# A recurrence followed by two MLPs: a deeper first-MLP pipeline, recurrence operations bound to their tiles, and low weight halves formed in PSUM

## The chip, the cores and the metric

The kernel runs on one core of a Trainium2 chip. The metric is the device time of one execution in microseconds (us), here the median of several. A core has five engines that run their own instruction streams, each in its own order, and wait for each other by semaphores: PE (matrix products; its weight loads are shown apart as PEld), DVE (elementwise), ACT (activation functions, copies), POOL (elementwise, slower), and SP, which here only issues DMAs. PE's clock is granted at one of two levels, 1.2 or 2.4 GHz; the profile gives the mean granted share of a stretch (1.00 is 2.4 GHz throughout).

## What is computed

A complex diagonal recurrence over 768 positions (4 batches of 8 heads, width 48), then two MLPs over the 3072 tokens of width 384. The first has a rational function of its hidden layer (2048 wide), the second a SiLU gate (1536 wide).

```python
for t in range(S):                                   # S = 768, states D x D, D = 48
    new_re = ar * S_re - ai * S_im
    new_im = ar * S_im + ai * S_re
    S_re, S_im = new_re + k_t v_t^T, new_im
    y[t] = q_t S_re
x = y reshaped to (3072, 384)
h = x @ w_in                                         # 384 -> 2048
P = a0 + a1 h + a2 h^2 + a3 h^3
Q = 1 + |b0| |h| + |b1| h^2
x = (P / (Q + 1e-6)) @ w_out                         # 2048 -> 384
g, val = x @ w_gate, x @ w_val                       # 384 -> 1536
out = (silu(g) * val) @ w_out                        # 1536 -> 384
```

## The kernel before

The tokens are worked in six passes of 512. A pass `i` is one call of `moe`: **stage A** is the first MLP, a loop over 16 blocks `f` of 128 hidden rows (L202 to L237), **stage B** the second MLP, a loop over 12 blocks (L249 to L267). Every product is made of three fp32r products: each operand stands as a high half and a low half (`hi`, `lo`), and high by high, high by low and low by high are summed. So a block of A costs PE 9 matmuls of 512 columns to form `ph` (`up`, L175) and 9 to add to the three accumulators `acc` (`down`, L183: six with `hi`, then three with `lo`). A block of B costs 18 for `pg` and `pv` and 9 for `acc`.

Between `up` and `down` of a block of A stand, with `ph` in PSUM: ACT `w` = |b1 ph| (L211) and `u` = a3 ph + a2 (L212); DVE `w` (L218, called p below), `u` (L221), ACT |w| (L222), DVE `u` (L223); ACT `Ln` and `Exp` (L117) that make the reciprocal `r`; and then the division, `divide`: DVE `hi` (L228), `w` (L229), `u` (L230) and POOL `lo` (L231). `half` and `pend` are lists that hold a block back: with `HALF` = 1 a block's division is written in the next block's turn, ahead of that block's own L218, and its `down` one turn later; L220 orders p behind the division. A block of B has ACT Silu, DVE `z` (L261), ACT `hi` (L262), DVE `lo` (L265).

Beside this runs the work for the next passes. The recurrence of a pair of units (512 tokens) is `ew_seed`, `ew_scan`, `ew_q`, `ew_k`, 36 steps in all (`EW`), almost all of it on DVE; its results go to DRAM (`qs`) and come back as `st`. `at_pair` then makes the 512 tokens of the next pass out of them with small matmuls (`pk`, `pp`, `pgs`, `py`, `px`), which is called attention here. `tick` is called once a block and issues some of these steps. How many, is set by the tables `ENDS` (recurrence done by the end of A and of B, in units of 36 steps), `SPAN` (blocks of A over which A's share is spread), `AT` (blocks over which attention is spread) and `HOLD` (attention steps held for the end of A). A scheduler then orders each engine's instructions by written order, readiness and its own costs; an `order(later, earlier)` binds two instructions of one engine.

The weights come as float64 words. `narrow` (L134) makes high and low halves of a block of 768 columns: three DVE bit operations (`to_bits`), ACT `hi`, two ACT operations for a range test, DVE `lo` = x - hi (L141). The halves are used in pass 0 and stored (`w1s`, `w2s`); later passes load them (`stored`, L290) into buffers of one tag, six of them (`W_BUFS`). Nine of the 16 blocks of the first MLP are converted before pass 0 (`EARLY1`), between the steps of the first pair's recurrence and attention. Other buffers: `ps` has 5 PSUM banks for everything but `acc`; `u` and `w` have 3, `r`, `hi` and `lo` 2. Ln and Exp share one ACT table (`lnexp`), Silu has another (`silu`); the table is switched with ACT_TABLE_LOAD.

## Time and profile before

| | |
|---|---|
| device time, median of 3 runs | 1451.88 us (1448.75 to 1460.53) |
| the profiled execution | 1443.08 us, its span 1441.2 us |
| PE matmul busy | 1149.0 us, 80% of the span |
| DVE busy | 987.0 us, 68% |
| ACT busy | 699.1 us, 49% |
| POOL busy | 127.3 us, 9% |
| DMA, mean over the span | 181 GB/s |

The busy share is a mean over stages that differ, so the span is cut below into stages: the time before the first `ph` matmul, and then A and B of each pass, cut at the first `ph` and the first `pg` matmul of each pass, to whole us. Passes 0, 1, 2, 4 and 5 are cut in two, pass 3 is one stretch. A matmul's shown length is modelled and longer than the distance at which matmuls follow each other; where a rate is wanted, it is taken from start to start.

### The profile page before, as it was taken

Reading aid. Unit: us, or ns where it says so; the run is one execution under the profiler, and the core shown is the slowest. Engines: PE = TensorE matmul, PEld = TensorE weight load, DVE = VectorE, ACT = ScalarE, POOL = GpSimd, SP = SyncE. Lnnn points to the kernel's source line nnn. Section 1 sums busy time; section 2 is a strip of 40 time slices with the busy share of each in tenths; the row PEclk is TensorE's granted clock in tenths of the full one; section 3 lists DMA queues with packets and bytes.
Section 4 is the critical chain, followed back from the end, with each engine's and each line's share of the span. In section 5 each row is a group of like instructions: output and inputs, shape, how many; then the busy total and the mean of one; then the engine's idle time right before and its main releaser. Section 6 shows DMA issues by size and latency. Waiting matters only on the chain.

```text
span 1441.2 us, 15114 instructions
## 1 busy us (share of the span) xinstructions
PE 1149.0 (80%) x5314; PEld 916.1 (64%) x5314; DVE 987.0 (68%) x1601; ACT 699.1 (49%) x1081; POOL 127.3 (9%) x110
## 2 busy tenths in 40 slices
PE   0047268579996788997889997899988989977797
PEld 0047135358884576885677875777867778854486
DVE  5967997998877888438887358879266752266521
ACT  6263478665466643238443258443254542354412
POOL 0000011110001111001111001110001110021100
PEclk9996599669899999999888999899999999999899
DMA  5386477556677744777334975336864346533451
GB/s 227 110 232 206 175 252 246 191 187 224 204 248 245 250 138 130 231 239 227 115 112 136 282 225 161 115 100 201 274 195 146 116 151 195 180 109 131 132 175 47
DMA packets 128291, 261.51 MB, mean 181 GB/s; under 512 B 8016, under 2 KB 85072, under 8 KB 127440
## 3 DMA queue, kind: packets, MB, share of 16 engines
q1 hardware_dynamic: 128208, 260.47, 55.8%
q8 instruction: 44, 0.72, 0.2%
q14 instruction: 39, 0.32, 0.1%
HBM read 210.11 MB, written 50.33 MB: 181 GB/s over the span
## 4 chain that ended last, share of the span: by engine, by line
PE 50%; DVE 21%; ACT 17%; POOL 5%; DMA 4%; issue 3%; POOLq 0%; SPq 0%; ACTq 0%; DVEq 0%
ACT r L117 5%; POOL lo L231 5%; PE acc L190 5%; PE acc L186 5%; PE acc L187 4%; PE pg L179 4%; PE pg L180 4%; PE pg L181 4%; PE pv L179 3%; PE pv L180 3%; PE pv L181 3%; PE py L646 3%; DVE hi L228 3%; DVE u L230 3%; ACT u L212 3%
## 5 line engine op out<-in xcount | busy, mean ns | idle before, releaser
L186 PE MATMUL acc<-hi,wt 128*128 128x512 f32 x504 | 220.6, 438 | 69.0 <-DVE hi L228 68.8
L231 POOL TENSOR_TENSOR lo<-u,r 128x512 fp32r<-128x512 f32 x96 | 126.6, 1319 | 1229.8 <-DVE u L230 1088.1
L187 PE MATMUL acc<-hi,wt 128*128 128x512 f32 x504 | 212.3, 421 | 0.0
L190 PE MATMUL acc<-lo,wt 128*128 128x512 f32 x504 | 159.2, 425 | 59.4 <-POOL lo L231 58.9
L261 DVE TENSOR_TENSOR w<-pv,u 128x512 f32<-128x512 f32 x72 | 49.8, 691 | 190.8 <-PE pv L181 190.7
L186 PEld LDWEIGHTS acc<-hi,wt 128*128 128x128 f32 x504 | 102.5, 203 | 114.6 <-DVE hi L228 93.2
L179 PE MATMUL ph<-xh,wt 128*128 128x512 f32 x288 | 124.4, 432 | 49.0 <-ACT wt L138 35.7
L190 PEld LDWEIGHTS acc<-lo,wt 128*128 128x128 f32 x504 | 93.0, 198 | 105.6 <-POOL lo L231 90.8
L211 ACT ACTIVATE w<-ph,par 128x512 f32<-128x512 f32 x96 | 65.9, 686 | 157.5 <-DVE u L230 132.5
L228 DVE SCALAR_TENSOR_TENSOR hi<-u,par,r 128x512 fp32r<-128x512 f32 x96 | 71.9, 749 | 92.9 <-ACT r L117 92.4
L181 PE MATMUL ph<-xh,wt 128*128 128x512 f32 x288 | 119.0, 413 | 2.9 <-DVE wt L141 2.9
L180 PE MATMUL ph<-xl,wt 128*128 128x512 f32 x288 | 118.8, 412 | 0.0
L117 ACT ACTIVATE u<-pg 128x512 f32<-128x512 f32 x72 | 43.0, 598 | 154.9 <-PE pg L181 154.9
L187 PEld LDWEIGHTS acc<-hi,wt 128*128 128x128 f32 x504 | 103.1, 205 | 19.5
L262 ACT ACTIVATE hi<-w 128x512 fp32r<-128x512 f32 x72 | 45.4, 630 | 124.8 <-DVE w L261 124.5
L179 PEld LDWEIGHTS ph<-xh,wt 128*128 128x128 f32 x288 | 58.2, 202 | 72.6 <-ACT wt L138 38.9
L619 PE MATMUL pk<-ident,st 96*128 96x96 f32 x160 | 23.8, 275 | 92.5 <-DMA st<-qs 91.8
L212 ACT ACTIVATE u<-ph,par 128x512 f32<-128x512 f32 x96 | 74.7, 778 | 40.7 <-POOL lo L231 40.5
L179 PE MATMUL pg<-x1h,wt 128*128 128x512 f32 x216 | 89.0, 412 | 1.1 <-ACT x1h L122 1.1
L180 PE MATMUL pg<-x1l,wt 128*128 128x512 f32 x216 | 86.7, 401 | 0.0
L181 PE MATMUL pg<-x1h,wt 128*128 128x512 f32 x216 | 86.4, 400 | 0.0
L179 PE MATMUL pv<-x1h,wt 128*128 128x512 f32 x216 | 85.0, 393 | 0.0
(110 smaller groups left out, 2513.0 us busy)
## 6 DMA issues: line engine op xcount, KB each, us to landing
wt<-w1s SPq DMA_DIRECT2D x89, 768.0 KB, 4.4
wt<-w2s SPq DMA_DIRECT2D x60, 768.0 KB, 4.6
wt<-w2s SPq DMA_DIRECT2D x60, 384.0 KB, 4.1
raw<-in_w_p SPq DMA_DIRECT2D x28, 768.0 KB, 5.6
qs<-qp SPq DMA_DIRECT2D x24, 768.0 KB, 5.0
st<-qs SPq DMA_DIRECT2D x96, 192.0 KB, 5.1
w1s<-wt SPq DMA_DIRECT2D x16, 768.0 KB, 4.1
a<-in_a_p SPq DMA_DIRECT2D x6, 1536.0 KB, 8.9
```

Of the source, the lines that this page charges most:

```text
L117: i = act(*args, **kw)
L179: t_.matmul(ph, whi, xh[:, k, :], start=(k == 0), stop=False)
L180: t_.matmul(ph, whi, xl[:, k, :], start=False, stop=False)
L181: t_.matmul(ph, wlo, xh[:, k, :], start=False, stop=(k == KT - 1))
L186: t_.matmul(acc[m], wt[:, 0, c : c + 128], hi, start=st, stop=False)
L187: t_.matmul(acc[m], wt[:, 1, c : c + 128], hi, start=False, stop=False)
L190: t_.matmul(acc[m], wt[:, 0, c : c + 128], lo, start=False, stop=sp)
L211: act(w, ph, AF.Abs, scale=b1)
L212: act(u, ph, AF.Identity, scale=a3, bias=a2)
L228: stt(hi, u, a0, r, ADD, MUL)
L231: g_.tensor_tensor(lo, u, r, MUL)
L261: tt(z, pv, sg, MUL)
```

## The change

Three things are changed.

First, in A the division of a block is written behind the next block's own DVE work (`order(half.pop(0)(), formed)`), where it stood ahead of it, and `flush(gf)` leaves one block more between a division and its `down`. `hi` and `lo` are now taken from their buffers inside `divide`. p is ordered behind the last division (`divided[-1]`).

Second, `tt` and `stt` are wrapped (`held_back`, one line of the file, so all of DVE's tensor operations show as that line): while `tick` runs, each of them is ordered behind the DVE operation `formed` of the block in which it is issued. Before, the scheduler could run such an operation as soon as its inputs were there. `ENDS`, `SPAN` and `AT` are changed with it: in passes 1 to 3, B now ends with whole pairs done (3.0, 4.0, 5.0 where it was 2.8, 3.8, 4.8), and attention of passes 2 to 4 begins at block 1 of A.

Third, for the first MLP's weights the low half is formed by PE: in PSUM, x times the identity minus hi times the identity, 384 columns at a time, and ACT copies it to `lo`.

```diff
-ENDS = ((1.06, 1.5), (2.06, 2.8), (3.06, 3.8), (4.06, 4.8), (5.0, 5.0), (5.0, 5.0))
-SPAN = (16, 10, 5, 5, 5, 5)
-AT = ((16, 16, 0, 11), (10, 16, 0, 6), (4, 16, 0, 1), (4, 16, 0, 1), (4, 16, 0, 1), (4, 16, 0, 1))
+ENDS = ((1.06, 1.5), (2.06, 3.0), (3.06, 4.0), (4.06, 5.0), (5.0, 5.0), (5.0, 5.0))
+SPAN = (16, 11, 8, 8, 5, 5)
+AT = ((16, 16, 0, 11), (12, 16, 0, 6), (1, 16, 0, 1), (1, 16, 0, 1), (1, 16, 0, 1), (1, 16, 0, 1))
...
-    tt, stt, act = v_.tensor_tensor, v_.scalar_tensor_tensor, s_.activation
+    act = s_.activation
+    pin = {"on": False, "at": None}
+    def held_back(op):
+        def f(*args, **kw):
+            i = op(*args, **kw)
+            if pin["on"] and pin["at"] is not None:
+                order(i, pin["at"])
+            return i
+        return f
+    tt, stt = held_back(v_.tensor_tensor), held_back(v_.scalar_tensor_tensor)
...
+    minus = cpool.tile([128, 128], F32R, name="minus")
-    def narrow(raw, x, wt, low_sum):
+    def narrow(raw, x, wt, low_sum, ps=None):
...
-        tt(lo, xf, hi.bitcast(F32), SUB)
+        if ps is None:
+            tt(lo, xf, hi.bitcast(F32), SUB)
+            return
+        n = lo.shape[1]
+        for c in range(0, n, DM):
+            d = ps.tile([128, DM], F32, tag="ps", name="d")
+            t_.matmul(d, ident, xf[:, c : c + DM], start=True, stop=False)
+            t_.matmul(d, minus, hi[:, c : c + DM], start=False, stop=True)
+            act(lo[:, c : c + DM], d, AF.Copy)
...
-            hi, lo = mt("hi", F32R), mt("lo", F32R)
             act(w, ph, AF.Abs, scale=b1)
             act(u, ph, AF.Identity, scale=a3, bias=a2)
-            if len(half) > HALF - 1:
-                flush(0)
-                last = half.pop(0)()
-            else:
-                last = None
             p = stt(w, w, b0, ph, ADD, MUL)
-            if last is not None:
-                order(p, last)
+            if divided:
+                order(p, divided[-1])
             tt(u, u, ph, MUL)
             act(w, w, AF.Abs)
-            stt(u, u, a1, ph, ADD, MUL)
+            formed = stt(u, u, a1, ph, ADD, MUL)
...
-            def divide(f=f, wts=wts, u=u, w=w, r=r, hi=hi, lo=lo):
-                stt(hi, u, a0, r, ADD, MUL)
+            def divide(f=f, wts=wts, u=u, w=w, r=r):
+                hi, lo = mt("hi", F32R), mt("lo", F32R)
+                first = stt(hi, u, a0, r, ADD, MUL)
                 stt(w, w, 1.0 + EPS, hi.bitcast(F32), ADD, MUL)
-                last = stt(u, u, a0, w, ADD, SUB)
+                divided.append(stt(u, u, a0, w, ADD, SUB))
                 g_.tensor_tensor(lo, u, r, MUL)
...
-            tick(0)
+            tick(0, formed)
+            if len(half) > HALF:
+                flush(gf)
+                order(half.pop(0)(), formed)
         while half:
-            flush(0)
+            flush(gf)
             half.pop(0)()
...
-            tt(z, pv, sg, MUL)
+            formed = tt(z, pv, sg, MUL)
...
-            tick(1)
+            tick(1, formed)
...
-            narrow(raw, x, wt, bad_of)
+            narrow(raw, x, wt, bad_of, conv_ps[0] if src is w1_p else None)
...
+                pin["on"], pin["at"] = True, ins
                 cnt[ph] += 1
...
+                pin["on"] = False
```

How the instructions stand now is seen at three places. The first is DVE in A of pass 5, where no other work runs; numbers tell blocks apart. Before, the three operations of a division (`hi`, `w`, `u`) and the three of the next block (with `ph`) alternate, and a division uses the `u` of the block just formed:

```order
L218 SCALAR_TENSOR_TENSOR w_9035<-w_9035,par_90,ph_9022 128x512
L221 TENSOR_TENSOR u_9034<-u_9034,ph_9022 128x512
L223 SCALAR_TENSOR_TENSOR u_9034<-u_9034,par_90,ph_9022 128x512
L228 SCALAR_TENSOR_TENSOR hi_9037<-u_9034,par_90,r_9036 128x512
L229 SCALAR_TENSOR_TENSOR w_9035<-w_9035,hi_9037 128x512
L230 SCALAR_TENSOR_TENSOR u_9034<-u_9034,par_90,w_9035 128x512
```

In the changed kernel the division between the blocks 9131 and 9169 is that of the block before 9131 (`u_9105`); the one of `u_9143` comes after the next block:

```order
L87 SCALAR_TENSOR_TENSOR w_9144<-w_9144,par_90,ph_9131 128x512
L87 TENSOR_TENSOR u_9143<-u_9143,ph_9131 128x512
L87 SCALAR_TENSOR_TENSOR u_9143<-u_9143,par_90,ph_9131 128x512
L87 SCALAR_TENSOR_TENSOR hi_9163<-u_9105,par_90,r_9107 128x512
L87 SCALAR_TENSOR_TENSOR w_9106<-w_9106,hi_9163 128x512
L87 SCALAR_TENSOR_TENSOR u_9105<-u_9105,par_90,w_9106 128x512
L87 SCALAR_TENSOR_TENSOR w_9182<-w_9182,par_90,ph_9169 128x512
L87 TENSOR_TENSOR u_9181<-u_9181,ph_9169 128x512
L87 SCALAR_TENSOR_TENSOR u_9181<-u_9181,par_90,ph_9169 128x512
L87 SCALAR_TENSOR_TENSOR hi_9201<-u_9143,par_90,r_9145 128x512
```

The same six operations stand in the same proportion; what moved is which block a division belongs to.

The second is DVE in B of pass 2, at its third to sixth block: `w<-pv` is `z`, `lo` the low half, the rest is the recurrence. Before, this stretch held the last of it, and from the fifth block on B had none:

```order
L261 TENSOR_TENSOR w_5273<-pv_5249,u_5272 128x512
L531 TENSOR_TENSOR qp_5700<-q_5698,a_4421 128x8x6x16
L265 TENSOR_TENSOR lo_5275<-w_5273,hi_5274 128x512
L531 TENSOR_TENSOR qp_5700<-q_5698,a_4421 128x8x6x16
L531 TENSOR_TENSOR qp_5744<-q_5742,a_4421 128x8x6x16 x2
L567 TENSOR_TENSOR t6_5751<-t6_5751 128x8x96
L261 TENSOR_TENSOR w_5318<-pv_5294,u_5317 128x512
L567 TENSOR_TENSOR t6_5808<-t6_5808 128x8x96
L265 TENSOR_TENSOR lo_5320<-w_5318,hi_5319 128x512
L261 TENSOR_TENSOR w_5369<-pv_5345,u_5368 128x512
L265 TENSOR_TENSOR lo_5371<-w_5369,hi_5370 128x512
L261 TENSOR_TENSOR w_5416<-pv_5392,u_5415 128x512
```

In the changed kernel it is the beginning of the recurrence, and it goes on in this density to the last block:

```order
L87 TENSOR_TENSOR w_5391<-pv_5367,u_5390 128x512
L87 SCALAR_TENSOR_TENSOR t2_5358<-t1_4697,t2_5358 128x4x192
L87 TENSOR_TENSOR t3_5408<-a_4480 128x768
L87 TENSOR_TENSOR a_4480<-a_4480,t2_5358 128x1536
L87 TENSOR_TENSOR a_4480<-t3_5408 128x192 x2
L87 TENSOR_TENSOR lo_5393<-w_5391,hi_5392 128x512
L87 TENSOR_TENSOR t3_5408<-a_4480 128x768
L87 TENSOR_TENSOR w_5441<-pv_5417,u_5440 128x512
L87 TENSOR_TENSOR a_4480<-t3_5408 128x192 x2
L87 TENSOR_TENSOR t3_5408<-a_4480 128x768
L87 TENSOR_TENSOR lo_5443<-w_5441,hi_5442 128x512
L87 TENSOR_TENSOR a_4480<-t3_5408 128x192 x2
```

So nearly all of a pair's recurrence moved from A into B.

The third is ACT near the end of B of pass 2, where the recurrence needs Ln and Exp (`t6`) while B uses Silu (`u<-pg`). Before, they stood behind the last Silu of the pass, after the one table load that the next A needs anyway:

```order
L262 ACTIVATE hi_5682<-w_5681 128x512
L117 ACTIVATE u_5726<-pg_5706 128x512
L104 ACT_TABLE_LOAD
L117 ACTIVATE t6_5751<-t6_5751,cst_91 128x8x96
L117 ACTIVATE t6_5808<-t6_5808,cst_91 128x8x96
L262 ACTIVATE hi_5728<-w_5727 128x512
L117 ACTIVATE t6_5751<-t6_5751 128x8x96
L117 ACTIVATE t6_5808<-t6_5808 128x8x96
```

In the changed kernel they stand between the tenth and the eleventh Silu, with a table load ahead of them and one behind:

```order
L131 ACTIVATE u_5775<-pg_5751 128x512
L588 ACTIVATE t6_5793<-a_4480 128x1536
L588 ACTIVATE t6_5798<-a_4480 128x1536
L118 ACT_TABLE_LOAD
L284 ACTIVATE hi_5777<-w_5776 128x512
L131 ACTIVATE t6_5793<-t6_5793,cst_91 128x8x96
L131 ACTIVATE t6_5798<-t6_5798,cst_91 128x8x96
L131 ACTIVATE t6_5793<-t6_5793 128x8x96
L131 ACTIVATE t6_5798<-t6_5798 128x8x96
L118 ACT_TABLE_LOAD
L131 ACTIVATE u_5828<-pg_5808 128x512
```

Two loads are added by this in each of passes 1 to 3, six in all. On PE of pass 5 the `down` of a block stands about four blocks behind its `up`; in passes 2 to 4 three blocks.

## Rows read from the trace of the kernel before

**Rows 1.** Stretches: length; busy (count) of PE, PEld, DVE, ACT, POOL; clock; DMA share, GB/s.
```profile
0.00:163.00 163.00, 43.97 (x269) 43.15 (x270) 128.50 (x236) 75.10 (x106) 0.71 (x14) 0.87 0.57 191
163.00:309.00 146.00, 96.53 (x288) 63.41 (x288) 133.08 (x183) 101.13 (x153) 24.05 (x16) 0.76 0.66 220
309.00:422.00 113.00, 113.00 (x615) 97.77 (x615) 93.10 (x180) 63.64 (x118) 0.00 (x0) 0.90 0.60 202
422.00:558.00 136.00, 104.41 (x463) 78.89 (x461) 112.48 (x178) 81.28 (x120) 20.47 (x16) 0.91 0.64 211
558.00:640.00 82.00, 81.78 (x405) 68.95 (x405) 39.70 (x72) 23.69 (x37) 0.00 (x0) 1.00 0.70 214
640.00:778.00 138.00, 115.91 (x563) 92.69 (x561) 110.99 (x195) 78.49 (x125) 20.52 (x16) 0.90 0.47 150
778.00:850.00 72.00, 71.80 (x318) 59.47 (x319) 33.58 (x43) 21.57 (x33) 0.00 (x0) 1.00 0.77 237
850.00:1055.00 205.00, 186.22 (x912) 151.10 (x911) 147.05 (x246) 99.60 (x154) 20.50 (x16) 0.95 0.56 177
1055.00:1176.00 121.00, 106.14 (x549) 85.06 (x547) 83.68 (x120) 62.78 (x100) 20.53 (x16) 0.96 0.46 148
1176.00:1250.00 74.00, 73.78 (x328) 60.90 (x327) 18.96 (x28) 17.93 (x29) 0.00 (x0) 1.00 0.61 192
1250.00:1359.00 109.00, 81.57 (x291) 53.65 (x289) 67.26 (x96) 56.29 (x85) 20.52 (x16) 0.95 0.37 123
1359.00:1441.00 82.00, 73.87 (x326) 61.11 (x326) 18.65 (x28) 17.58 (x30) 0.00 (x0) 0.98 0.37 117
```
**Rows 2.** Timeline of pass 5, A, one block: start, length, instruction, [idle before <- releaser].
```profile
1330.84 0.75 DVE L228 SCALAR_TENSOR_TENSOR hi<-u,par,r 128x512 fp32r<-128x512 f32 x1 [2.20 <-ACT r L117]
...
1331.62 0.69 DVE L229 SCALAR_TENSOR_TENSOR w<-w,hi 128x512 f32<-128x512 f32 x1
...
1332.35 0.75 DVE L230 SCALAR_TENSOR_TENSOR u<-u,par,w 128x512 f32<-128x512 f32 x1
...
1333.02 0.74 DVE L218 SCALAR_TENSOR_TENSOR w<-w,par,ph 128x512 f32<-128x512 f32 x1
...
1333.27 1.27 POOL L231 TENSOR_TENSOR lo<-u,r 128x512 fp32r<-128x512 f32 x1 [5.22 <-DVE u L230]
1333.68 0.68 DVE L221 TENSOR_TENSOR u<-u,ph 128x512 f32<-128x512 f32 x1
1334.39 0.75 DVE L223 SCALAR_TENSOR_TENSOR u<-u,par,ph 128x512 f32<-128x512 f32 x1
...
1335.26 0.62 ACT L222 ACTIVATE w<-w 128x512 f32<-128x512 f32 x1
...
1336.66 0.63 ACT L117 ACTIVATE r<-r 128x512 f32<-128x512 f32 x1
1337.32 0.75 DVE L228 SCALAR_TENSOR_TENSOR hi<-u,par,r 128x512 fp32r<-128x512 f32 x1 [2.18 <-ACT r L117]
```

**Rows 3.** Timeline of PE in pass 3, A, a dense stretch; eight matmuls of 512 columns.
```profile
893.21 0.40 PE L180 MATMUL ph<-xl,wt 128*128 128x512 f32 x1
...
894.81 0.39 PE L181 MATMUL ph<-xh,wt 128*128 128x512 f32 x1
```

**Rows 4.** Waits in pass 5, A: who <- for whom: us in total, times, longest.
```profile
DVE hi L228 <- ACT r L117: 33.3, 16, 3.1
```

**Rows 5.** Waits in the first 163 us.
```profile
PE ph L179 <- ACT wt L138: 26.5, 1, 26.5
```

**Rows 6.** Weight loads of L290, all 209 of them, from issue to landing.
```profile
DMA to landing us min/median/max: 3.5/4.5/8.2
```

**Rows 7.** Groups by line and shape: count, busy us, mean ns, idle before.
```profile
L117 ACT ACTIVATE t<-t,cst 128x768 f32<-128x768 f32 x36 | 33.0, 930 | 1.7 <-DVE t L567 1.7
...
L141 DVE TENSOR_TENSOR wt<-raw,wt 128x768 fp32r<-128x768 f32 x28 | 26.7, 954 | 1.2 <-ACT wt L138 1.0
...
L104 ACT ACT_TABLE_LOAD x12 | 15.4, 1283 | 0.9 <-PEq L857 0.7
```

More of the change, by code (lines that the diff above doesn't have):

```diff
@@ L193, in mt @@
             return mp.tile([128, gf, T], dt, tag=tag, name=tag, bufs=M_BUFS.get(tag, 3))
-        pend, half = [], []
+        pend, half, divided = [], [], []
         def flush(n):
@@ L233, in divide @@
                     pend.append((acc, wts[j], DM, hi[:, j, :], lo[:, j, :], f + j == 0, f + j == F1 - 1))
-                return last
+                return first
             half.append(divide)
-            tick(0)
+            tick(0, formed)
+            if len(half) > HALF:
+                flush(gf)
+                order(half.pop(0)(), formed)
         while half:
-            flush(0)
+            flush(gf)
             half.pop(0)()
-        tick(2)
+        tick(2, None)
         flush(0)
@@ L309, in spans @@
         return [(c, min(2 * DM, src.shape[2] - c)) for c in range(0, src.shape[2], 2 * DM)]
-    ntiny = [0]
+    ntiny, conv_ps = [0], [None]
     def moe_pools(es):
@@ L417, in general @@
                     split(px, xh[:, :, cs], xl[:, :, cs])
-                moe(pools, 512, xh, xl, out[:, :, bass.ds(j * (UPB * 512) + k * 512, 512)], lambda ph: None, silu, feed(stored, pools[3]))
+                moe(pools, 512, xh, xl, out[:, :, bass.ds(j * (UPB * 512) + k * 512, 512)], lambda ph, ins: None, silu, feed(stored, pools[3]))
     with ExitStack() as es:
@@ L721, in tile_recurrence_moe @@
         lnexp()
+        conv_ps[0] = ps
         run(ew_seed(0))
+        nc.sync.dma_start(ident, ident_p)
+        act(minus, ident, AF.Copy, scale=-1.0)
         nc.sync.dma_start(mask, mask_p)
-        nc.sync.dma_start(ident, ident_p)
         nc.sync.dma_start(par[:, 0:4], ma.partition_broadcast(128))
@@ L749, in at_to, with tick @@
                     next(at, None)
-            def tick(ph, cnt=[0, 0], eb=eb, e0=e0, e1=e1, n=n, at=at, at_to=at_to, at_n=at_n, w=AT[i], i=i):
+            def tick(ph, ins, cnt=[0, 0], eb=eb, e0=e0, e1=e1, n=n, at=at, at_to=at_to, at_n=at_n, w=AT[i], i=i):
                 if ph == 2:
```

## Prediction

> **What bounds the kernel now.** I read the stretches first [rows 1], because the mean shares (PE 80%, DVE 68%) hide that the stages differ. B of pass 4 takes 74 us with PE busy 73.78 at clock 1.00 and DVE at 18.96: PE and nothing else. A of pass 5 has the same shape of work without company, and takes 109 us with PE 81.57 and DVE 67.26: neither engine is full. What a matmul of 512 columns costs at full clock comes from the dense stretch [rows 3]: seven distances in 1.60 us, 0.229 us each. So PE needs 324 x 0.229 = 74 us for a B, which it gets, and 288 x 0.229 = 66 us for an A, which takes 109 to 138.
>
> The timeline of A says why [rows 2]. From one `hi` to the next is 6.48 us, and it is one chain: `hi`, `w`, `u` of the division on DVE, then p (1333.02), then |w|, Ln and Exp on ACT (Exp ends 1337.29), then the next `hi` (1337.32). DVE stands 2.2 us before each `hi`; over the stage it waits 33.3 us for ACT's `r` in 16 waits [rows 4]. PE could do the block's 18 matmuls in 4.1 us. So A is bound by a latency loop between DVE and ACT, not by any engine. In passes 1 to 3 the recurrence sits on DVE in the same stage (111 to 112 us of 136 to 138 [rows 1]).
>
> **The deeper pipeline, bare (pass 5).** With the division one block behind, ACT's Abs, Ln and Exp run while DVE does the other block's division. The loop is then DVE's six operations at their distances [rows 2]: p 0.66, `u` 0.71, `u` to `hi` 0.67 (not shown in this order; taken as the distance from `u` to p, 0.67, and at most the dependent distance 0.78), `hi` 0.78, `w` 0.73, `u` 0.67: 4.22 us, against PE's 4.11. Sixteen blocks are 68 us, ahead of them about 3 (9 matmuls, 2.1, and a first ACT operation, 0.7), behind them about 5 (POOL `lo` 1.27 [rows 2], three matmuls 0.7, and the split of `acc`, two operations of some 0.7 twice over): 76 us where 109 stand. **Gain 33.** What is late next is the weights: the six buffers of the tag are now held for up to four or five blocks, so a load starts only when a `down` ends, and it has about one block of PE time to land. Landing takes 4.5 in the median and 8.2 at most [rows 6]. Two blocks cost at least a landing and a block of PE: (4.5 + 4.1)/2 = 4.3 us, nothing; with 8.2, 6.15 us a block and no more than 5 us gained in all. I take the median, since nothing else loads in pass 5 (0.37 of the DMA engines busy).
>
> **A of passes 2 to 4.** PE's attention work: pass 4's A has 258 matmuls more than pass 5's and 24.6 us more of PE [rows 1]. So PE needs 66 + 25 = 91 us. DVE's recurrence r and attention a: pass 2 has 36 steps and 144.6 us of DVE in A and B, pass 5 has neither and 85.9, pass 4 has a fifth of the steps and 102.6. So r + a = 58.7 and 0.2 r + a = 16.7; r = 52.5, a = 6.2. With two of 36 steps left in A, DVE needs 67.3 + 2.9 + 6.2 = 76 us. PE bounds, and with 2 us at the start and 7 for the tail and the waits of `pk` for `st` (the last products are now written at the end of B, shortly before they are read back), A takes 100. Below lies PE's 91, above 120, if attention's hand-overs between PE, ACT and DVE keep today's idle time. Gains: pass 2, 138 to 100, **38**; pass 3, whose A was 205 - 72 = 133, **33**; pass 4, 121 to 100, **21**.
>
> At this place the busy shares mislead. PE is shown busy 115.9 of 138 us in A of pass 2, which would leave 22 us to win; counted by starts 47 are left. By the busy time the idle of PE in the A stages of passes 1 to 5 is 32 + 22 + 19 + 15 + 27 = 115 us, less the 33 that B gives back below: 1361 us as profiled. The Trainium skill, "Perfetto Trace Analysis", section "Identifying the Most-Contended Engine", says that matmul busy share does not tell how near PE is to its limit and LDWEIGHTS share does. The trace agrees: PEld is busy 92.7 of 138 there, 45 us short [rows 1].
>
> **What B gives back.** B of passes 1 to 3 gets 34 of 36 steps, 49.6 us of DVE, on its own 18.7: 68 us against PE's 74. It fits, narrowly, but `z` and `lo` of a block now queue on DVE behind pieces of 4.1 us, and PE is only one block ahead. In addition Ln and Exp come between two Silus: two table loads of 1.28 and four operations of some 0.9 [rows 7], 6.2 us in which no `z` can start, against the 4.1 us of matmuls that PE has ready. I take 82 where 72 stand, **minus 10** each in passes 2 and 3. Bounds: 74, if all of it hides, and 123, if each piece is exposed (12 x (6.17 + 4.13)).
>
> **Pass 1.** A has 20 steps: DVE 67.3 + 29.2 + 3 = 99, and 11 for start and tail, 110 where 136 stand: gain 26. B has PE's 82 and some 6 more of attention, and DVE's 71: 95 where 82 stand. **Gain 13.**
>
> **The weights and pass 0.** DVE loses 16 operations of 0.954 [rows 7], 15.3 us. PE gains 32 pairs of 384 columns. A single pass is 0.17 us; if fp32 takes up to four passes at half clock, 1.4, and 0.2 to 0.3 for the other: 12 to 54 us in all, in stretches where PE is idle 119 and 50 us [rows 1]. ACT gains 32 copies of some 0.5 us (half the columns of the 0.93 operation), 16 us where it is busy 176 of 309. So these are hidden, unless PE's order puts them ahead of attention. For the gain: the stretch before the first `ph` ends with PE waiting 26.5 us for the first converted weights [rows 5], which queue on DVE behind the next pair's recurrence. Bound to its tiles, that recurrence no longer stands ahead of them. Against it: DVE has then less to fill its gaps before 163 us and more to do in A of pass 0, where it is busy 133 of 146. I set the two against each other: **0**, between 15 gained and 15 lost.
>
> **The sum** against the profiled 1443.1 us: 0 + 13 + (38 - 10) + (33 - 10) + 21 + 33 = 118, so 1325. The runs' median is 0.6% above that execution (1451.9), so I predict 1.006 x 1325 = **1333 us**.
>
> **The rivals.**
> *Loads or hand-overs take part of it* (chance 0.17). Six buffers are just enough, and landings near 8.2 would make pass 5's A 105 and cost pass 1 some 14: 1325 + 43 = 1368, 1376 on the runs' scale. The same result comes from A of passes 2 to 4 at 115. For it: the loads wait for `down` already today. Against: in passes 2 to 4 `down` is three blocks behind, which leaves a load two blocks and attention, some 11 us.
> *All of it hides* (0.15). B stays at PE's 74, that is 8 us better than taken in three passes, pass 0 gains 15, and A of 2 to 4 comes at 95: 1325 - 24 - 15 - 15 = 1271, 1279. For it: by DVE's sum there is room.
> *Slower* (0.04). The one mechanism is B of passes 1 to 3: if neither the pieces nor `z` and `lo` lie beside PE's matmuls, a block costs 6.17 + (49.6 + 18.7)/12 = 11.9 us and a B 142; three of them are 180 us over the forecast, 1513. It decides from about 124 us a B, where each recurrence piece is exposed whole. Against it: `ps` has five banks, and a block takes two, so PE works a block ahead.
> *The change does nothing* (0.02): the scheduler could have undone the order. The order of the built kernel shows the division a block later and the recurrence in B, so only a new wait of the same length in A could bring this.
>
> **How the numbers follow.** The forecast has 0.62, and its own bounds (95 to 108 for an A, 76 to 90 for a B, 15 either way in pass 0) reach from 1290 to 1370. To leave out no more than 2 in 10 the range goes to 1275 below, near the second rival, and to 1395 above, past the first. One per cent, about 15 us, is what a measurement of this kernel can tell from no change. Faster by more: 0.62 + 0.17 + 0.15 = 0.94; within 1%: 0.02; slower: 0.04.
>
> **What would show it.** In pass 5's A: `hi` waits for `r` no more, blocks follow at 4.2 to 4.4 us, clock near 1.00. In passes 2 to 4: PE waits for no `hi`, A near 100. In B of passes 1 to 3: DVE near 70 us of busy time, and waits of PE for `lo` and of ACT's Silu behind a table load; 82 us. The forecast is wrong if PE's first wait in A is for a weight load (above 5 us a block), if B exceeds 95, or if the first `ph` starts later than 163 us.

## The result, and the profile after

The changed kernel takes 1370.05 us (median of 4 runs, 1363.92 to 1378.43) where the kernel before took 1455.05 beside it: a ratio of 0.942, 95% interval 0.935 to 0.949. That is faster by 5.8%, inside the range of 1275 to 1395, 37 us above the number 1333 and 6 us from the first rival's 1376. The profiled execution took 1367.86 us, its span 1366.0.

The stretches of after, cut as [rows 1] at the first `ph` and the first `pg` of each pass. Columns: stretch, length; busy time and count of PE, PEld, DVE, ACT, POOL; granted clock; DMA share, GB/s.

```profile
0.00:167.80 167.80, 78.25 (x341) 56.74 (x342) 92.04 (x152) 77.71 (x120) 0.72 (x14) 0.75 0.60 202
167.80:345.20 177.40, 105.98 (x313) 71.59 (x311) 144.49 (x235) 104.84 (x160) 23.54 (x16) 0.73 0.47 151
345.20:453.20 108.00, 104.76 (x615) 89.89 (x616) 91.24 (x157) 72.18 (x130) 0.00 (x0) 1.00 0.73 252
453.20:575.50 122.30, 94.44 (x406) 74.61 (x405) 101.27 (x167) 77.52 (x117) 20.79 (x16) 0.87 0.65 211
575.50:662.30 86.80, 86.80 (x457) 74.20 (x458) 67.24 (x126) 29.50 (x42) 0.00 (x0) 1.00 0.60 192
662.30:769.80 107.50, 103.38 (x566) 88.39 (x565) 81.21 (x121) 74.15 (x122) 20.91 (x16) 0.94 0.63 207
769.80:841.40 71.60, 71.59 (x315) 58.81 (x316) 63.60 (x119) 27.07 (x37) 0.00 (x0) 1.00 0.69 219
841.40:956.30 114.90, 110.78 (x598) 95.98 (x596) 81.84 (x123) 74.41 (x120) 20.88 (x16) 0.90 0.57 179
956.30:1027.80 71.50, 71.48 (x315) 58.81 (x316) 64.48 (x125) 27.07 (x37) 0.00 (x0) 1.00 0.69 221
1027.80:1131.40 103.60, 100.84 (x550) 86.50 (x549) 79.43 (x117) 60.50 (x98) 20.84 (x16) 0.95 0.59 188
1131.40:1205.40 74.00, 73.97 (x328) 61.27 (x329) 18.96 (x28) 17.79 (x29) 0.00 (x0) 1.00 0.60 193
1205.40:1284.00 78.60, 69.73 (x290) 54.10 (x288) 65.75 (x97) 55.66 (x86) 20.94 (x16) 0.98 0.49 166
1284.00:1366.00 82.00, 73.81 (x326) 61.07 (x326) 18.60 (x28) 17.33 (x29) 0.00 (x0) 0.97 0.38 121
```

Read against [rows 1]: A of passes 1, 2, 4 and 5 lost 14, 31, 17 and 30 us (122.3 for 136, 107.5 for 138, 103.6 for 121, 78.6 for 109), pass 3 as a whole 19 (186.4 for 205). The recurrence has left A: DVE is busy 81 us there in pass 2 where it was 111, and 64 us in the B behind it where it was 34. B of pass 2 did not get longer (71.6 for 72), B of pass 1 did, by 5 (86.8 for 82). And one place lost: the first `pg` comes at 345 us where it came at 309. The change gained some 111 us behind that point and gave 36 back ahead of it.

The latency loop is gone exactly as worked out. A timeline of DVE in pass 5's A, one block (start, length, instruction), to be held against [rows 2]:

```profile
1240.16 0.75 DVE L87 SCALAR_TENSOR_TENSOR hi<-u,par,r 128x512 fp32r<-128x512 f32 x1
1240.94 0.69 DVE L87 SCALAR_TENSOR_TENSOR w<-w,hi 128x512 f32<-128x512 f32 x1
1241.67 0.75 DVE L87 SCALAR_TENSOR_TENSOR u<-u,par,w 128x512 f32<-128x512 f32 x1
1242.34 0.74 DVE L87 SCALAR_TENSOR_TENSOR w<-w,par,ph 128x512 f32<-128x512 f32 x1
1243.00 0.68 DVE L87 TENSOR_TENSOR u<-u,ph 128x512 f32<-128x512 f32 x1
1243.72 0.75 DVE L87 SCALAR_TENSOR_TENSOR u<-u,par,ph 128x512 f32<-128x512 f32 x1
1244.38 0.75 DVE L87 SCALAR_TENSOR_TENSOR hi<-u,par,r 128x512 fp32r<-128x512 f32 x1
```

From `hi` to `hi` are 4.22 us where 6.48 were, with no wait in any of the six rows. (All of DVE's two-input operations now have one line, L87, that of the helper that binds them; they are told apart by their tiles.)

What grew ahead of 345 us shows in the waits and groups. The waits of PE and of SP's queue in the first 168 us, PE's largest wait in A of pass 0, and the page's group of the first product for `d` (32 products; each of these shows as two instructions, so x64). Columns of a wait: us, times, longest; of a group: busy, mean ns | idle before:

```profile
PE d L163 <- DVE raw L87: 66.2, 9, 18.3
...
SPq L326 <- ACT wt L165: 85.8, 11, 13.8
...
PE acc L210 <- DVE hi L87: 40.9, 8, 8.9
...
L163 PE MATMUL d<-raw,ident 128*128 128x384 f32 x64 | 42.2, 774 | 71.2 <-DVE raw L87 69.4
```

PE works in order. While it stands before a `d` product, what is written behind it stands too; and SP's queue stands 86 us before the store of a converted block (L326), whose low half `d` must form first, with the next loads of raw words behind it. How much of the 66 us costs time is settled below: 53 of them lie ahead of the first attention product.

### The profile page after: what moved, and what is told of

It is laid out like the page before. It is cut to its first block, busy times and chain, and to the rows that moved or that the text cites. A ratio compares the mean times of both kernels' runs of the same rounds, so it can differ in the third digit from the quotient of the medians.

```text
span 1366.0 us, 15421 instructions
## 1 busy us (share of the span) xinstructions
PE 1145.8 (84%) x5410; PEld 932.0 (68%) x5410; DVE 970.2 (71%) x1585; ACT 715.7 (52%) x1120; POOL 128.6 (9%) x110
## 4 chain that ended last, share of the span: by engine, by line
PE 66%; DVE 16%; DMA 7%; ACT 7%; issue 3%; POOL 1%; SPq 0%; POOLq 0%; ACTq 0%; DVEq 0%
PE acc L214 7%; PE acc L210 7%; PE acc L211 7%; PE pg L203 4%; PE pg L205 4%; DMA wt<-w1s 4%; PE pg L204 4%; PE pv L203 4%; PE pv L204 4%; PE pv L205 3%; DVE t L87 3%; PE py L668 3%; PE ph L203 3%; PE pp L645 3%; PE ph L204 3%
## 5 line engine op out<-in xcount | busy, mean ns | idle before, releaser
L210 PE MATMUL acc<-hi,wt 128*128 128x512 f32 x504 | 217.1, 431 | 53.4 <-DVE hi L87 53.4
L211 PE MATMUL acc<-hi,wt 128*128 128x512 f32 x504 | 210.8, 418 | 0.0
L214 PE MATMUL acc<-lo,wt 128*128 128x512 f32 x504 | 155.1, 416 | 23.3 <-POOL lo L250 23.3
L203 PE MATMUL ph<-xh,wt 128*128 128x512 f32 x288 | 119.1, 414 | 32.2 <-DMA wt<-w1s 26.8
L87 DVE TENSOR_TENSOR w<-pv,u 128x512 f32<-128x512 f32 x72 | 49.6, 689 | 126.9 <-PE pv L205 112.7
L214 PEld LDWEIGHTS acc<-lo,wt 128*128 128x128 f32 x504 | 97.6, 199 | 52.3 <-POOL lo L250 31.6
L87 DVE SCALAR_TENSOR_TENSOR w<-w,par,ph 128x512 f32<-128x512 f32 x96 | 71.5, 744 | 63.6 <-ACT u L235 63.5
L205 PE MATMUL ph<-xh,wt 128*128 128x512 f32 x288 | 115.9, 402 | 0.0
L163 PE MATMUL d<-raw,ident 128*128 128x384 f32 x64 | 42.2, 774 | 71.2 <-DVE raw L87 69.4
L203 PE MATMUL pg<-x1h,wt 128*128 128x512 f32 x216 | 85.9, 398 | 3.5 <-ACT wt L154 2.0
L235 ACT ACTIVATE u<-ph,par 128x512 f32<-128x512 f32 x96 | 74.3, 774 | 20.2 <-POOL lo L250 20.1
L205 PE MATMUL pg<-x1h,wt 128*128 128x512 f32 x216 | 84.3, 390 | 0.3 <-DVE wt L87 0.3
```

Source lines behind the costliest of these rows:

```text
L87: i = op(*args, **kw)
L203: t_.matmul(ph, whi, xh[:, k, :], start=(k == 0), stop=False)
L205: t_.matmul(ph, wlo, xh[:, k, :], start=False, stop=(k == KT - 1))
L210: t_.matmul(acc[m], wt[:, 0, c : c + 128], hi, start=st, stop=False)
L211: t_.matmul(acc[m], wt[:, 1, c : c + 128], hi, start=False, stop=False)
L214: t_.matmul(acc[m], wt[:, 0, c : c + 128], lo, start=False, stop=sp)
```

## The experiments

All stages below are cut like the ones above, in us, each from one profiled execution; "to `pg` 0" is the time up to the first `pg` of pass 0. The first two rows are the two kernels, the others the experiments that change the parts. In the expectations and below, TensorE is PE, VectorE is DVE and ScalarE is ACT.

| kernel | to `pg` 0 | B0 | A1 | B1 | A2 | B2 | A3 | B3 | pass 4 | pass 5 |
|---|---|---|---|---|---|---|---|---|---|---|
| before | 309.0 | 113.4 | 135.9 | 81.7 | 138.2 | 71.9 | 133.5 | 71.9 | 194.9 | 190.8 |
| after | 345.2 | 108.0 | 122.2 | 86.9 | 107.5 | 71.6 | 114.9 | 71.5 | 177.5 | 160.6 |
| depth alone | 300.7 | 109.5 | 122.3 | 81.7 | 116.3 | 71.9 | 118.3 | 71.9 | 180.4 | 161.2 |
| depth, tables | 299.4 | 106.4 | 124.8 | 89.2 | 112.4 | 71.9 | 123.1 | 74.3 | 176.5 | 160.2 |
| depth, tables, bound in 2, 3 | 300.2 | 106.3 | 118.7 | 87.6 | 98.9 | 71.6 | 117.9 | 71.5 | 174.6 | 161.4 |
| after, lows on DVE | 319.9 | 109.6 | 122.4 | 86.9 | 107.5 | 71.6 | 114.9 | 71.5 | 174.4 | 161.4 |
| after, not bound | 328.7 | 106.6 | 106.2 | 87.9 | 112.2 | 71.9 | 121.0 | 74.5 | 171.3 | 160.6 |
| after, bound from pass 1 | 333.8 | 110.0 | 121.0 | 86.9 | 107.5 | 71.6 | 117.9 | 71.5 | 177.6 | 162.0 |
| after, old division | 338.6 | 114.1 | 125.6 | 86.9 | 115.9 | 71.6 | 120.9 | 72.2 | 190.5 | 190.5 |
| before, lows on PE | 325.9 | 112.1 | 124.9 | 83.3 | 134.0 | 71.9 | 138.7 | 71.9 | 193.5 | 192.3 |

**The first part undone.**

```diff
+            if half:
+                flush(0)
+                half.pop(0)()
             p = stt(w, w, b0, ph, ADD, MUL)
...
-            if len(half) > HALF:
-                flush(gf)
-                order(half.pop(0)(), formed)
```

> The changed kernel with its first part undone: in A the division of the block before stands again ahead of p, `down` follows it at once, and `hi` waits for `r` one block earlier; binding, tables and TensorE's low halves stay. My theory (the latency loop between VectorE and ScalarE bounded A, 6.48 us a block): A of pass 5 goes from 79 back to 105 to 110, A of passes 2 to 4 from 104 to 115 back to 112 to 125 (16 blocks at 6.5 to 7), pass 1 some 10 us longer: total 1410 to 1450. Rival (the recurrence's move out of A is what brought passes 2 to 4, and TensorE's attention work there fills the loop's gaps): only pass 5 loses 30 us, passes 1 to 4 stay within 5 us each, total 1390 to 1405.

Measured: 1433.63 us, ratio to before 0.990 (0.987 to 0.994). So without the deeper division binding, tables and TensorE's low halves together bring 1% (13 us), and the division is worth 64 us on top. The waits of DVE in A of pass 5 and of pass 2 show the old loop back:

```profile
DVE hi L87 <- ACT r L131: 33.3, 16, 3.3
...
DVE hi L87 <- ACT r L131: 24.0, 15, 4.4
```

The first line is [rows 4] again, the sum to the tenth, and A of pass 5 is 108.6 us. My theory holds in passes 2 to 4 (A of 116 to 121) and in pass 5. It missed pass 1, whose A is 3 us longer where some 10 were expected. The rival (attention fills the loop's gaps) does not hold: A of passes 2 to 4 is 6 to 13 us longer, not within 5.

**The first part alone.** The kernel of the separate losses (below) with the three old tables.

```diff
-ENDS = ((1.06, 1.5), (2.06, 3.0), (3.06, 4.0), (4.06, 5.0), (5.0, 5.0), (5.0, 5.0))
-SPAN = (16, 11, 8, 8, 5, 5)
+ENDS = ((1.06, 1.5), (2.06, 2.8), (3.06, 3.8), (4.06, 4.8), (5.0, 5.0), (5.0, 5.0))
+SPAN = (16, 10, 5, 5, 5, 5)
(AT likewise)
```

> The kernel before with the deeper division alone: old tables, no recurrence bound, low halves on VectorE. Question: what does the first part bring by itself, and what the new tables bring on top (that kernel, with the new tables, took 1339 us). Theory (the recurrence in A is VectorE's load there and must leave before the deeper division pays): pass 5 gains its 30 us, passes 2 and 3 gain 10 to 20 each (VectorE's 111 us in A are then the bound), pass 1 10, total 1355 to 1385. Rival (depth alone brings it, the tables nothing): 1332 to 1348.

Measured: 1331.10 us, 0.916 (0.912 to 0.920), 1 us below the rival's range. On the total the rival was right and my theory wrong: the deeper division alone does it, and the rest of the change takes some 39 us of that away again (1370.05 less 1331.10, each beside its own runs of before). By stages the theory was nearer than by its total: A of passes 2 and 3 gained 22 and 15 us, where it said 10 to 20; it had left out A of pass 4 (15) and the stretches up to A of pass 1 (12). What the new tables alone bring on top is unclear: with them the kernel took 1338.86 us, and the intervals overlap. A of pass 2 of this kernel:

```profile
614.20:730.50 116.30, 103.69 (x564) 85.22 (x562) 101.93 (x146) 77.39 (x126) 21.77 (x16) 0.94 0.57 181
```

DVE still carries 102 us there. That is more than after's 81, but it is under PE's 104, so it mostly hides, and the recurrence need not leave A for the division to pay. The two parts overlap, though: with the old division, binding and tables took A of pass 2 from 138 to 116 us as well. That is why the division is worth 118 us alone and only 64 on top of the rest.

**The third part undone.**

```diff
-            narrow(raw, x, wt, bad_of, conv_ps[0] if src is w1_p else None)
+            narrow(raw, x, wt, bad_of, None)
```

> The changed kernel with its third part undone: the 32 low halves of the first MLP's weights are formed by one subtraction each on VectorE again, and TensorE has no `d`. Question: where do the 31 us come from that pass 0 lost (first `ph` at 168 instead of 163, A 177 instead of 146). Theory P (the `d` matmuls stand in TensorE's order behind `down` and ahead of the next `ph`, so that conversion and VectorE go in lock-step): pass 0 comes back by 15 to 30 us, first `ph` at 160 to 165, total 1337 to 1352. Rival R (the recurrence that is bound to its tiles leaves VectorE idle before the first `ph` and loads it in A): VectorE only gets 15 us more to do, pass 0 is 5 to 20 us longer, total 1371 to 1386. Passes 1 to 5 the same to 2 us by both.

**The second part undone.** (The binding holds whatever VectorE does within a `tick`, attention's operations too; these runs do not part the two. Up to B of pass 0 only recurrence is issued there.)

```diff
-                pin["on"], pin["at"] = True, ins
+                pin["on"], pin["at"] = False, ins
```

> The changed kernel without the binding of the recurrence to its tiles (the order that each `tick` puts on VectorE's recurrence operations is never set); order of the division, tables and TensorE's low halves as changed. Theory R (the bound recurrence is pass 0's loss): first `ph` near 163, A of pass 0 near 150, 25 us gained there; and in passes 1 to 3 the recurrence slides out of B back into A, where VectorE's gaps are, and A of passes 2 and 3 becomes 10 to 20 us longer each: total 1350 to 1385. Rival P (TensorE's `d`): pass 0 stays at about 345 us to the first `pg`, total 1375 to 1410. Third view (the tables alone place the recurrence, the binding does little): passes 1 to 5 the same to 3 us each.

**The second part from pass 1 on**, with `i > 0` in that place.

> The changed kernel with the recurrence bound to its tiles only from pass 1 on, so that VectorE may fill the stretch before the first `ph` and pass 0 with recurrence as before. Theory R: A of pass 0 comes from 177 to about 150 and the first `ph` to 163 or less, total 1336 to 1350. Rival P (TensorE's `d` in the conversion): pass 0 stays within 8 us of the changed kernel's, total 1358 to 1370. If both bear a part, between them, 1350 to 1358.

**The second and third part undone together.**

> The changed kernel without its second and third part together: VectorE forms the low halves, no recurrence is bound, the deeper division and the new tables stay. Theory S (the two losses are separate and add up: TensorE's low halves cost 26 us and the binding 22, as each alone showed): first `ph` and A of pass 0 together 300 to 312 (before 309, changed 345), A of pass 1 near 106, total 1315 to 1330. Rival O (both cost the same thing, the lock-step of conversion and attention before the first `ph`, and one undone has undone it): 1338 to 1348.

Measured: lows on DVE 1343.76 us, 0.929 (0.923 to 0.934); not bound 1348.35, 0.932 (0.928 to 0.936); bound from pass 1 1354.16, 0.934 (0.929 to 0.939); both undone 1338.86, 0.923 (0.917 to 0.928). Each of the four is faster than the change by its median; for the second and third the interval touches that of the change (0.935 to 0.949). Of three of them, the stretches before the first `ph` and A of pass 0, in the order lows on DVE, not bound, both undone:

```profile
0.00:149.00 149.00, 37.81 (x268) 37.15 (x268) 94.55 (x155) 61.67 (x89) 0.71 (x14) 0.92 0.61 207
149.00:320.00 171.00, 101.65 (x289) 67.13 (x289) 156.01 (x248) 106.03 (x160) 24.67 (x16) 0.72 0.52 173
```
```profile
0.00:186.40 186.40, 81.84 (x340) 58.95 (x341) 140.24 (x249) 96.83 (x144) 0.71 (x14) 0.71 0.58 195
186.40:328.70 142.30, 94.81 (x313) 67.64 (x312) 119.07 (x183) 92.30 (x144) 27.25 (x16) 0.80 0.56 184
```
```profile
0.00:162.60 162.60, 43.79 (x269) 42.96 (x269) 128.15 (x236) 75.30 (x107) 0.71 (x14) 0.87 0.56 191
162.60:299.40 136.80, 94.65 (x288) 65.16 (x288) 130.04 (x175) 97.99 (x150) 25.71 (x16) 0.76 0.70 229
```

These, with after's two rows, make a square, read at the first `pg`. With TensorE's low halves: 345.2 bound, 328.7 unbound. With VectorE's: 319.9 and 299.4. So the low halves on PE cost 25 us (bound) or 29 (unbound), the binding 16 or 20, and the two add up to within 4 us. The binding's part is DVE's: it keeps some 34 us of recurrence out of the stretch before the first `ph` (94.6 us of DVE instead of 128.2). The first `ph` comes 13 us earlier for it, as I had argued, and A of pass 0 then holds 156 us of DVE in 171 and is 34 us longer. TensorE's part shifts the first `ph`, from 149 to 168 or from 163 to 186. Two waits of the first of the three kernels, in its first 149 us, show what PE's idle time there is made of:

```profile
PE pk L641 <- DMA st<-qs: 91.6, 1, 91.6
...
SPq L326 <- DVE wt L87: 62.5, 8, 12.5
```

With the low halves on DVE, PE's idle time ahead of attention is one wait, for the first `st`; behind it attention runs in one piece, and then PE waits 18.8 us for the first `ph`. With `d`, five of PE's nine waits for DVE (53 of the 66 us) lie in the place of that first wait and cost nothing: the first `pk` starts at 88.5 us, where it starts at 91.6 without `d`. The loss comes behind it, where the last of the early blocks are converted between the pieces of attention (`CV`). From the first `pk` to the end of the last `px`, with `d` (the changed kernel) and without (its low halves on DVE):

```profile
88.49:146.28 57.79, 47.47 (x287) 42.59 (x288) 17.86 (x25) 21.55 (x39) 0.00 (x0) 0.71 0.63 198
91.62:130.57 38.95, 37.80 (x268) 37.12 (x268) 14.64 (x21) 13.03 (x25) 0.00 (x0) 0.93 0.66 203
```

PE is busy 9.7 us longer, which is the products of `d` (9.6 us there; attention's own take 38 in both), and idle 9.2 us longer. These 19 us are the whole delay of the first `ph` (18.4 us); A of pass 0, which has `d` of its own, is another 7 longer. The clock of the second row, 0.93, can't be right and is no other cause: eight `pp` take 1.97 us up to 107 us in that kernel and 1.08 behind, the same two lengths as in the changed one. The stores that SP's queue puts ahead of the next loads wait 86 us instead of 70 (the 62.5 shown and one of 7.0 put down to another DVE operation).

Of the expectations, theory P was right for the low halves on DVE (25 us, total 1344), though the first `ph` came at 149 us, earlier than the 160 to 165 that it gave. For the binding the total fell just below the lower end given, and I was wrong about the place: the first `ph` went to 186, not to 163, since the lock-step with `d` stays; A of passes 2 and 3 grew by 5 and 6 us, not 10 to 20, and A of pass 1 shrank by 16, which no theory had. Bound from pass 1 on, the kernel lies where both bear a part, 1354, and its stretches say the same: the first `ph` at 193.9, late by `d`, and A of pass 0 139.8, as without binding. For "both undone" theory S holds up to the first `pg` (299.4 us for 300 to 312), but the total came as rival O said, because A of pass 1 went the other way: 124.8 instead of the 106.2 of the unbound kernel.

**The third part alone, on the kernel before** (old division, old tables, nothing bound).

> The kernel before with the third part alone: TensorE forms the low halves of the first MLP's weights and ScalarE copies them; old division, old tables, nothing bound. The step of my prediction that is tested: the 64 `d` pairs are hidden in TensorE's idle time of the first 309 us (119 and 50 us), so nothing. Theory P (TensorE works in order; its `d` wait for the converted bits, and attention stands behind them): first `ph` 15 to 25 us later, first `ph` and A of pass 0 together 325 to 340 instead of 309, total 1465 to 1480. Rival H (hidden, as forecast; the loss came only with the rest of the change): within 6 us of 1450.

Measured: 1450.91 us, 1.003 (0.999 to 1.007): no difference. Each theory was right about half of it. The first `ph` is 27 us late, at 189.5, and the first `pg` 17 us late, as P said; the end is not late, as H said. The first two stretches, and A of pass 1:

```profile
0.00:189.50 189.50, 85.11 (x340) 62.28 (x341) 142.48 (x251) 96.72 (x144) 0.72 (x14) 0.62 0.58 192
189.50:326.00 136.50, 93.59 (x314) 62.63 (x313) 121.05 (x209) 94.89 (x148) 23.66 (x16) 0.85 0.59 193
...
438.00:563.00 125.00, 99.69 (x462) 76.18 (x460) 109.26 (x191) 76.05 (x117) 20.45 (x16) 0.95 0.65 206
```

DVE used the longer wait for recurrence (142 us of work ahead of the first `ph`, before 128), A of pass 0 is shorter by 10, and A of pass 1 by another 11, at a granted clock of 0.95 instead of 0.91 [rows 1]. The unbound kernel shows the same: A of pass 1 is 106 us with TensorE's low halves and 125 without. Why that stage gives the loss back when nothing is bound, I can't say: in one pair the waits for weight loads fell (18.2 to 7.6 us), in the other they hardly did (7.9 to 7.2). It stays open.

**The recurrence bound in passes 2 and 3 alone**, with the low halves on DVE.

```diff
-                pin["on"], pin["at"] = True, ins
+                pin["on"], pin["at"] = i in (2, 3), ins
```

> As the kernel of the separate losses (VectorE forms the low halves, deeper division, new tables), and the recurrence bound to its tiles in passes 2 and 3 alone, where the bound kernel's A and B were 11 to 14 us shorter in sum than the unbound one's. Theory (the binding keeps A of 2 and 3 free of recurrence, and costs only where VectorE needs it as filling, in passes 0 and 1): 8 to 14 us below the kernel without any binding, total 1302 to 1320. Rival (what is kept out of A there comes back in the next stage, or passes 2 and 3 differ only by chance): within 4 us of the kernel without binding.

Measured: 1311.69 us, 0.903 (0.894 to 0.911), 27 us below the kernel without binding, where 8 to 14 were expected. In the two profiled executions, 29 us apart, 22 lie in passes 2 and 3 and 8 in pass 1, which is bound in neither kernel; those 8 no theory had. No kernel here is faster; by the medians it is 19 us below the deeper division alone. A of pass 2, B of pass 2, A of pass 3:

```profile
613.00:712.00 99.00, 96.80 (x563) 82.03 (x563) 75.86 (x113) 72.55 (x121) 20.95 (x16) 1.00 0.64 210
712.00:783.00 71.00, 71.00 (x314) 58.34 (x313) 63.00 (x119) 26.74 (x37) 0.00 (x0) 1.00 0.68 218
783.00:901.00 118.00, 114.03 (x599) 98.73 (x597) 82.07 (x122) 74.36 (x119) 20.88 (x16) 0.87 0.55 174
```

A of pass 2 is 99 us where the forecast said 100, with PE busy 96.8. A of pass 3 has 36 more matmuls and takes 118, and PE idles 4 us in it: what is left is the clock, 0.87. By [rows 1] and these rows the stage costs PE the same work at two speeds: a clock of 0.87 over 118 us is 31 us at the lower level (2 x 0.13 x 118), half of which, 15, is lost, and 103 would remain. The same sum gives 103 from after's 114.9 at 0.90, and 101 from after's A of pass 2, 107.5 at 0.94.

**No attention held back to the end of A; two pieces held instead of four; spread over A alone.** The first is on the changed kernel, the other two on the kernel bound in passes 2 and 3.

```diff
-HOLD = (0, 3, 4, 4, 4, 0)
+HOLD = (0, 0, 0, 0, 0, 0)      first
+HOLD = (0, 3, 2, 2, 2, 0)      second
+HOLD = (0, 3, 0, 0, 0, 0)      third, with AT (1, 16, 0, 0) for passes 2 to 4
```

> The changed kernel with no attention held back to the end of A (HOLD is 0 in all passes): the pieces of passes 1 to 4 are spread over A's blocks. Question: A of passes 2 and 3 took 108 and 115 us where 100 were forecast, TensorE waited only 4 us there, and its clock was at half for 13.8 and 24.0 us around the held pieces. Theory C (the small matmuls of two or more held pieces in a row bring the clock down, and `down` behind them pays): spread, A of pass 2 is near 102 and A of pass 3 near 104, granted clock 0.97 or more, total 1345 to 1360. Rival W (the pieces cost their half clock wherever they stand, or bring waits of `ph` and `down` for their hand-overs between the blocks): A of passes 2 and 3 within 4 us of before or longer, total 1366 to 1385.

> The kernel bound in passes 2 and 3 (1312 us), with 2 instead of 4 pieces of attention held to the end of A in passes 2 to 4. By theory C (the run of held pieces sets the half clock) the stretches at half clock behind A's last products get shorter: A of pass 3, 118 us with 30.6 us at half clock, comes to 104 to 110; total 1298 to 1308. By rival W (half clock comes with small matmuls anywhere, and falls now here, now there) the sum of A of passes 2 to 4 stays within 6 us of 317; total 1306 to 1325.

> The kernel bound in passes 2 and 3 (1312 us), with the attention of passes 2 to 4 spread over the blocks of A alone: nothing held to its end and nothing left to B. Question: does what follows A's end at half clock come from the held pieces? Spread also into B, A of pass 3 was 110 us instead of 115 and each B 6 longer. Theory C (held pieces in a row bring the clock down and the `down` matmuls behind them pay): A of passes 2 and 3 at 97 to 103 with a granted clock of 0.97 or more, B at 71.6, total 1290 to 1308. Rival W (the half clock comes with the small matmuls wherever they stand): the sum of A of 2, 3 and 4, which was 317 us, within 6 us or longer, total 1308 to 1330.

Where the clock falls in after's A of pass 3 had suggested these. Two neighbouring stretches of it, ahead of its end:

```profile
921.00:937.60 16.60, 16.60 (x112) 14.74 (x111) 15.29 (x24) 10.05 (x16) 5.05 (x4) 1.00 0.59 191
937.60:954.60 17.00, 17.00 (x74) 15.84 (x73) 1.71 (x3) 1.65 (x4) 0.39 (x1) 0.50 0.09 24
```

In the 5 us ahead of the fall PE did `pgs` and `py`, products of 48 columns; in the 17 us behind it the rest of the held pieces and 13 of A's last `down` matmuls, all at the lower level, and without a gap. But theory C fell. With nothing held the time is 1392.76 us, 0.962 (0.956 to 0.968), 23 us more than the change by the medians and above what either theory said; A of pass 2 is 107.1 us at the same 0.94, A of pass 3 110.2 at 0.94, and each B from pass 1 to 4 is 4 to 6 us longer, for the part of attention that the table then sends there. With two held 1311.79 us, 0.903 (0.898 to 0.907): the same as with four; A of passes 2 to 4 is 312.5 us in sum (98.1, 112.9, 101.5) instead of 317.4, and A of pass 3 stays above the 104 to 110 of theory C. Spread over A alone 1317.10, 0.908 (0.904 to 0.913), with a sum of 323.3 (101.2, 113.5, 108.6), of which A of pass 2 lies where theory C put it and A of pass 3 does not. The lower clock comes with attention in some stages and stays away in others of the same work, held or spread. What tips it, the runs don't show.

**Two more operations on VectorE in each block of B**: `lo` is formed three times.

```diff
-            tt(lo, z, hi.bitcast(F32), SUB)
+            for _ in range(3):
+                tt(lo, z, hi.bitcast(F32), SUB)
```

> The changed kernel with two operations more on VectorE in each block of B: `lo` is formed three times from the same tiles, 24 times 0.685 us or 16.4 us more a B. Question: how near B of passes 1 to 3 is to giving something back. Theory D (VectorE's sum decides: 63 us of 71.6 today, so 79 to 80): B of passes 2 and 3 is 79 to 84 us (8 to 12 more each), B of pass 1 88 to 95, B of passes 4 and 5 the same to 1 us, total 1388 to 1402. Rival E (pieces are exposed in series with `z` and `lo`, as my 10 us a pass assumed): each block pays for its added 1.37 us, 16 more in each of B 1 to 3, total 1412 to 1425. Rival H (TensorE is far enough ahead, and the pieces slip into A): less than 3 us a B, total under 1380.

Measured: 1404.65 us, 0.967 (0.959 to 0.975), 35 more than the change. D's total (1388 to 1402) was nearly met, at another place. B of passes 2 and 3 got shorter, not longer, 68.2 and 68.0 us. DVE's last `w` and `lo` of B of pass 2 and PE's first `ph` of pass 3 show how:

```profile
862.16 0.39 PE L203 MATMUL ph<-xh,wt 128*128 128x512 f32 x1
...
874.35 0.68 DVE L87 TENSOR_TENSOR w<-pv,u 128x512 f32<-128x512 f32 x1
...
882.36 0.68 DVE L87 TENSOR_TENSOR lo<-w,hi 128x512 fp32r<-128x512 f32 x1
```

PE doesn't wait: it goes on with the next pass's `ph` and does B's last `down` products later. DVE falls 20 us behind and catches up in A. From the first `pg` of pass 1 to that of pass 5 the kernel is only 14 us longer, for four B's with 16.4 us more each; put on the three of them that hold recurrence it is some 5 us of 16. The other 21 are 18 ahead of it (13 of them in B of pass 0, 121.2 for 108.0, at a clock of 0.91 where it was 1.00) and 2.5 in the last B. So the recurrence in B has some 10 us or more to spare, and E, my own series of pieces, is refuted.

## Why the prediction was right, and where it was not

**The direction and the mechanism** were right: A was bound by the loop between DVE and ACT. Undoing the division alone brings the loop and 64 us back, and having it alone brings 118.

**Pass 5: right.** Forecast 4.22 us a block and 76 in all, a gain of 33; measured 4.22, 78.6 and 30. The median landing was the right one to take: `ph` waits 3.6 us in all for weight loads there.

**A of passes 2 to 4: the work was right, the clock was missing.** Forecast 100 each; measured 107.5, 114.9 and 103.6. PE's work is as worked out where the clock stays up (99 us for A of pass 2 in the kernel bound in passes 2 and 3, at 1.00 and with PE idle 2 us), and PE waits only 4, 4 and 3 us in the three. The rest is the lower clock, by the sum above, which is an estimate (101 and 103 us remain without it, and 98 in pass 4); the forecast took the clock as 1.00 throughout. [rows 1] had 0.90 for A of pass 2, and I put it all down to PE's waits. The first rival named 115 for these stages, but by hand-overs and loads, and those do not appear.

The forecast set PE's busy time aside and counted matmuls by their starts. On that the Trainium skill, "Perfetto Trace Analysis", section "Identifying the Most-Contended Engine", was cited: matmul busy share does not tell how near PE is to its limit, LDWEIGHTS share does. The trace agrees with the first half: a matmul is shown 0.39 us long where the next one starts 0.229 behind it [rows 3], so short gaps do not show, and a stage of 563 matmuls that was shown busy 115.9 us [rows 1] was done in 99 (up to 14 of these 17 us may be the clock's, 0.90 there and 1.00 here: half of 27.6 us). Of the second half it shows the bound: with PE full, PEld is busy 82.03 of 99, or 58.34 of 71, so 0.82 to 0.83 is full here, and not 1.

**B's give-back: wrong.** The step put 10 us a pass (82 for 72) on `z` and `lo` queueing behind pieces and on Ln and Exp between two Silus. Measured 71.6 and 71.5 us, so 20 us of the sum were charged for nothing. DVE's 63.6 of 71.6 us lie beside PE's matmuls, and the added operations showed that even 80 would, mostly, because PE passes over B's last `down` products into the next A. B of pass 1 took 86.9 for the 95 of the forecast, and its A 122 for 110, with 18 us of waits of `ph` for weight loads and a clock of 0.87: there the first rival's loads did take a part.

**The weights and pass 0: wrong, and the costliest step.** It said: hidden, since PE is idle 119 and 50 us there, and the binding's two effects cancel. Measured at the first `pg`: 36 us late, of which B of pass 0 gives 5 back (its clock was 1.00 where it was 0.90). By the square above, division and tables gained 10 us there, the binding lost 20, and the low halves on PE lost 25. The forecast's own sign of being wrong, a first `ph` later than 163 us, came true with 167.8. Of PE's 119 idle us, 92 were one wait for `st`. The `d` products that lie there are hidden, as forecast. Those of the blocks converted behind it are not: they stand among attention's products, whose stretch grows by 19 us, half products and half waits (the condition that the step itself named and did not price: "unless PE's order puts them ahead of attention"). The binding's gain ahead of the first `ph` (13) and its loss behind it (34) were both foreseen, and set equal without a sum, though [rows 1] had A of pass 0 at 133 of 146 us of DVE: what is added there comes out at the end.

**The total.** Forecast on the profiled scale 1325, measured 1368: 43 us, of which pass 0 makes 31, and passes 1 to 5 (gain 106 instead of 118) 12. In these 12 two errors offset each other: over the five passes A is 41 us longer than forecast and B 29 shorter. Of the rivals, the first gave the right time (1376) by causes that bear only A of pass 1; the second was right on B alone; the slower one needed B's of 124 us and none came near. That depth alone lands on 1331 is chance, and no merit of the sum.

## What to carry to other kernels

Find the loop that sets a stage's rate by the distance from one result to the same one a block later; a stage with two half-busy engines and such a loop gains from one more block of distance, and here that was the whole gain of the change. Work that is moved to an in-order engine "because it idles" must be placed where the idle time is: here `d` was free ahead of attention and cost 19 us in the midst of it. Price what stands behind it, also in the DMA queue. When a change has several parts, time each alone; here one part was worth 118 us alone, the others on top of it together minus 39 (without it they brought 13), and one of them, limited to the two passes that it suits, plus 27. What a part is worth depends on which others are there.

## What the runs showed of the hardware

The granted clock of the same stage differs from kernel to kernel. In the changed kernel, in the one bound in passes 2 and 3 alone, and in that one with attention spread over A, A of pass 2 ran at 0.94, 1.00 and 0.99, that of pass 3 at 0.90, 0.87 and 0.95, with PE idle 2 to 8 us in each. In a stage of about 100 us that is up to 15 us, as much as many a change; two kernels are compared stage by stage only with the clock beside the length. Products of 48 to 128 columns, back to back, stood ahead of falls to the lower level although PE had no gap (17.0 of 17.0 us shown busy at 0.50), so a busy PE row is no sign of full speed.
